# Scratch words of the integer conversions in one of three product banks, beside the first expert

## The chip, the cores and the metric

The kernel runs on one core of one Trainium2 chip. The metric is the device time of the whole program in microseconds (us), the median of three runs. The engines are PE (matmul), DVE (vector), ACT (scalar), POOL (GpSimd) and SP (which issues most DMAs). Each runs its own instructions in order and waits on semaphores for the others.

## The reference

Three layers follow one another: a linear attention with decay, a mixture of eight experts that each take exactly 384 tokens, and a dense layer with a rational function between its two products. Tokens are handed to experts greedily, best score first.

```python
for t in range(S):                                    # attention, S = 768, 4 x 8 heads of 64
    state = gamma * state + einsum('bhd,bhe->bhde', k[:, :, t], v[:, :, t])
    y[:, :, t] = scale * einsum('bhd,bhde->bhe', q[:, :, t], state)
...
for idx in np.argsort(-(x @ w_gate).flatten()):       # routing, cap = 3072 / 8 = 384
    tok, e = idx // E, idx % E
    if assigned[tok] < 0 and counts[e] < cap: assigned[tok] = e; counts[e] += 1
...
out[mask] = np.maximum(x[mask] @ w1[e], 0) @ w2[e]    # D = 512, F = 1024
...
h = x @ w_in                                          # 512 -> 2048
g = (a0 + a1*h + a2*h**2 + a3*h**3) / (1 + |b0|*|h| + |b1|*h**2 + 1e-6)
return g @ w_out                                      # 2048 -> 512
```

`w_in` and `w_out` arrive as 64-bit floats, and the kernel converts them to 32-bit words itself.

## The kernel before, in words

The attention and the gate run first (to about 190 us). The rest goes expert by expert, `n` = 0 to 7, and each expert's 384 tokens pass through all four products before the next expert's. An expert has three stages here. `xt` turns the gathered tokens round (three tiles). The first layer alternates `mm1(n, f)` and `mm2(n, f)` for eight blocks f, the third alternates `mm3(n, i)` and `mm4(n, i - 3)` for sixteen blocks i. Every 32-bit product is three matmuls of a high and a low part (`three`), and one product of this size is 12 matmuls.

Between the third and the fourth product lies the rational function: `rat1` (ACT L868 to L870, POOL L871, DVE L872 and L873), `rat2` (ACT L882, L883), `rat3` (DVE L888 to L890) and `gsplit` (ACT L895, POOL L896), which gives `mm4` its operand `hg`. DVE L873 is the last reader of the product that `mm3` left in PSUM.

PSUM has eight banks: `pr` for the routing, four `acc` for `mm2` and `mm4`, and three of the name "w", which `xt`, `mm1` and `mm3` take in turn.

Two more jobs run beside the first expert. The routing of the next expert is a chain of small steps that goes back and forth between DVE and PE in bank `pr` (L628 and L641 on PE, L635 to L637, L650, L583, L592 and L598 on DVE). And twelve blocks of `w_out` and `w_in` that weren't converted during the attention are converted now: six beside the first layer (`job_conv`, L949) and six beside the third (`in_conv_a`, L970). Twenty others were converted during the attention. One conversion (`conv`) is a shift and mask on DVE (L241), a scaled copy of the low words on ACT (L242), an OR on DVE (L243) and an addition on DVE (L244, in the rows as CUSTOM_DVE_ANT_0), after which ACT and POOL split the result (L247, L248). The conversions during the attention keep the intermediate word t1 in a PSUM tile `cvp`. The twelve beside the first expert keep it in SBUF, in the tile of the result (`xg` or `w2r`).

The order of PE, ACT and POOL is that of the code. The order of DVE and SP is made by a scheduler, which has its own idea of times and of when a buffer comes free.

## Time and profile before

| | |
|---|---|
| Time, median of 3 runs | 1081.24 us (1080.59 to 1082.49) |
| The profiled execution: its own time | 1081.6 us |
| Its span, first to last instruction | 1079.7 us |
| PE busy | 1010.1 us (94%) |
| DVE / ACT / POOL busy | 775.5 / 698.5 / 629.1 us |
| First expert: first layer | about 202 to 248 us |
| First expert: third layer | about 248 to 323 us |

The profile is one execution, some 0.4 us above the median. Starts in it are microseconds from the first instruction. In a row of the timeline, the bracket at the end is the idle time of that engine before the row and what ended it.

### The profile page before, as it was taken

What the parts mean: (1) busy time and instruction counts of PE and PEld (TensorE: products, weight loads), DVE (VectorE), ACT (ScalarE), POOL (GpSimd) and SP (SyncE); (2) the same over time, 40 slices, a digit from 0 to 9 for tenths busy, and PEclk for the clock granted to TensorE, in tenths of its full rate; (3) what the DMA queues carried; (4) which work ended last, traced back from release to release, by engine and by line L of the source; (5) the groups of instructions that cost most, each with busy time, mean ns of one, the idle gap of its engine ahead of it and who ended that gap; (6) DMA issues with size and microseconds to landing.
All of it is one profiled execution on the core that took longest, in us unless ns stands there. A gap on an engine that the chain in (4) does not pass through costs nothing.

```text
span 1079.7 us, 18280 instructions
## 1 busy us (share of the span) xinstructions
PE 1010.1 (94%) x6278; PEld 922.2 (85%) x6278; DVE 775.5 (72%) x1862; ACT 698.5 (65%) x1365; POOL 629.1 (58%) x612
## 2 busy tenths in 40 slices
PE   6999885679889999999999999999999999999995
PEld 5888774678779989998999899999998999989984
DVE  4899887678994788478747874787578756751773
ACT  6889882346684488458745874587358736873883
POOL 5677662464686367635663666366736663666452
PEclk9999997699999999999999999999999999999998
DMA  9999862523333212321232124212422142223110
GB/s 191 244 250 252 226 162 89 151 93 96 100 127 118 88 50 79 117 88 59 69 121 86 59 69 127 79 59 70 137 69 68 60 137 70 88 65 110 50 59 29
DMA packets 142028, 115.01 MB, mean 107 GB/s; under 512 B 56560, under 2 KB 122352, under 8 KB 141936
## 3 DMA queue, kind: packets, MB, share of 16 engines
q1 hardware_dynamic: 131184, 76.10, 26.7%
q0 software_dynamic: 10752, 37.75, 10.5%
q8 instruction: 49, 0.80, 0.3%
q14 instruction: 43, 0.35, 0.1%
HBM read 98.10 MB, written 15.73 MB: 105 GB/s over the span
## 4 chain that ended last, share of the span: by engine, by line
PE 63%; DVE 7%; ACT 2%; issue 2%; POOL 1%; POOLq 0%; DVEq 0%
PE w L814 30%; PE acc L910 22%; PE acc L814 8%; PE pr L628 1%; PE w L798 1%; DVE hg L825 1%; DVE cm L592 1%; ACT hg L824 0%; DVE t L872 0%; DVE t L890 0%; POOL qq L871 0%; DVE yT L842 0%; DVE qq L888 0%; DVE acc L889 0%; DVE pr L583 0%
## 5 line engine op out<-in xcount | busy, mean ns | idle before, releaser
L910 PE MATMUL acc<-woh,hg 128*128 128x512 f32 x1152 | 290.2, 397 | 4.8 <-ACT hg L895 4.5
L910 PEld LDWEIGHTS acc<-woh,hg 128*128 128x128 f32 x1152 | 212.8, 188 | 49.7 <-ACT hg L895 7.0
L871 POOL TENSOR_TENSOR qq<-qq,z 128x384 f32<-128x384 f32 x127 | 129.4, 1019 | 165.2 <-ACT z L869 163.7
L814 PE MATMUL w<-yT,wih 128*128 128x384 f32 x960 | 179.6, 339 | 0.1
L896 POOL TENSOR_TENSOR hg<-t,hg 128x384 fp32r<-128x384 f32 x127 | 131.6, 1037 | 81.4 <-ACT hg L895 53.1
L814 PEld LDWEIGHTS w<-yT,wih 128*128 128x128 f32 x960 | 166.4, 188 | 3.8 <-DVE yT L842 0.7
L814 PE MATMUL w<-xT,w1s 128*128 128x384 f32 x768 | 149.7, 343 | 0.6 <-ACT xT L800 0.6
L814 PE MATMUL acc<-hg,w2s 128*128 128x384 f32 x768 | 146.2, 339 | 0.3 <-DVE hg L825 0.3
L814 PEld LDWEIGHTS w<-xT,w1s 128*128 128x128 f32 x768 | 135.4, 192 | 1.9 <-ACT xT L800 0.8
L814 PEld LDWEIGHTS acc<-hg,w2s 128*128 128x128 f32 x768 | 132.7, 188 | 1.1 <-DVE hg L825 0.6
L888 DVE SCALAR_TENSOR_TENSOR qq<-qq,acc 128x384 f32<-128x384 f32 x128 | 70.8, 553 | 60.4 <-ACT acc L883 33.3
L248 POOL TENSOR_TENSOR w1s<-w1r,w1s 128x512 fp32r<-128x512 f32 x64 | 83.2, 1300 | 49.2 <-ACT w1s L247 48.4
L814 PE MATMUL w<-yT,wis 128*128 128x384 f32 x576 | 110.0, 339 | 1.1 <-DVE t L873 1.1
L248 POOL TENSOR_TENSOR w2s<-w2r,w2s 128x512 fp32r<-128x512 f32 x64 | 83.2, 1301 | 43.7 <-ACT w2s L247 43.4
L895 ACT ACTIVATE hg<-t 128x384 fp32r<-128x384 f32 x128 | 67.1, 525 | 63.9 <-DVE t L890 63.7
L814 PEld LDWEIGHTS w<-yT,wis 128*128 128x128 f32 x576 | 100.3, 188 | 3.7 <-DVE t L873 1.3
L868 ACT ACTIVATE qq<-w,rb 128x384 f32<-128x384 f32 x128 | 73.3, 573 | 36.9 <-PE w L814 35.6
L824 ACT ACTIVATE hg<-w 128x384 fp32r<-128x384 f32 x64 | 31.4, 490 | 92.1 <-PE w L814 92.1
L870 ACT ACTIVATE t<-w,ab 128x384 f32<-128x384 f32 x128 | 86.1, 673 | 0.0
L872 DVE TENSOR_TENSOR t<-w,t 128x384 f32<-128x384 f32 x128 | 70.4, 550 | 21.1 <-ACT t L870 21.1
L247 ACT ACTIVATE w2s<-w2r 128x512 fp32r<-128x512 f32 x64 | 40.2, 629 | 68.1 <-issue 41.7
L825 DVE SCALAR_TENSOR_TENSOR hg<-w,hg 128x384 fp32r<-128x384 f32 x64 | 35.6, 556 | 66.3 <-ACT hg L824 66.0
(183 smaller groups left out, 1761.7 us busy)
## 6 DMA issues: line engine op xcount, KB each, us to landing
wis<-wid POOLq DMA_DIRECT2D x42, 512.0 KB, 3.5
w1r<-in_moe_w_dram SPq DMA_DIRECT2D x64, 256.0 KB, 2.8
w2r<-in_moe_w_dram SPq DMA_DIRECT2D x64, 256.0 KB, 2.7
qn<-in_q_dram SPq DMA_DIRECT2D x48, 128.0 KB, 4.1
kn<-in_k_dram SPq DMA_DIRECT2D x24, 256.0 KB, 4.6
vn<-in_v_dram SPq DMA_DIRECT2D x24, 256.0 KB, 5.0
xd<-xn SPq DMA_DIRECT2D x48, 128.0 KB, 3.9
raw<-in_moe_w_in_dram SPq DMA_DIRECT2D x10, 512.0 KB, 6.5
```

The lines of the kernel that those rows point to most:

```text
L247: nc.scalar.activation(dst[:, 0], src, AF.Copy)
L248: lo_eng.tensor_tensor(dst[:, 1], src, dst[:, 0].bitcast(F32), op=OP.subtract)
L814: nc.tensor.matmul(o, w[a], x[b], start=first and n[key] == 1, stop=last and n[key] == total)
L825: HLO[n, f] = nc.vector.scalar_tensor_tensor(h[:, 1], p, 0.0, h[:, 0].bitcast(F32), op0=OP.max, op1=OP.subtract).ins
L868: nc.scalar.activation(qq, p, AF.Square, scale=rb)
L870: nc.scalar.activation(t, p, AF.Identity, bias=ab[:, 2:3], scale=ab[:, 3:4])
L871: light(n, i).tensor_tensor(qq, qq, z, op=OP.add)
L872: nc.vector.tensor_tensor(t, p, t, op=OP.mult)
L888: nc.vector.scalar_tensor_tensor(qq, qq, QC, r, op0=OP.add, op1=OP.mult)
L895: nc.scalar.activation(g[:, 0], t, AF.Copy)
L896: light(n, i).tensor_tensor(g[:, 1], t, g[:, 0].bitcast(F32), op=OP.subtract)
L910: nc.tensor.matmul(ACC[t], g[:, x, t * 128:(t + 1) * 128], woh[:, i, y], start=i == 0 and x + y == 0, stop=i == NF2 - 1 and x == 1)
```

## The change

The conversions beside the first expert put the intermediate word t1 into a PSUM tile of a new name, "x", with one buffer. The three product banks are now two of the name "w" and this one. While the first expert runs, `mm1` and `mm3` get "w" alone, and so take turns with two banks; the third tile of `xt(0)` and the tiles of `xt(1)` go to "x". From the second expert on, every third product goes to "x", so that products again take turns with three banks.

```diff
+    WN = [0]
+
+    def wtile(shape, first=False):
+        if not first:
+            WN[0] += 1
+        x = not first and WN[0] % 3 == 0
+        return ps.tile(shape, F32, name="x" if x else "w", bufs=1 if x else 2)
+
+    def ctile():
+        return ps.tile([128, 512], I32, name="x", bufs=1)
+
     def xt(n, t):
...
-        p = ps.tile([128, KD, 128], F32, name="w", bufs=3)
+        p = ps.tile([128, KD, 128], F32, name="x", bufs=1) if n == 1 else wtile([128, KD, 128])
...
     def mm1(n, f):
-        p = ps.tile([128, CAP], F32, name="w", bufs=3)
+        p = wtile([128, CAP], n == 0)
...
     def mm3(n, i):
-        p = US[n, i] = ps.tile([128, CAP], F32, name="w", bufs=3)
+        p = US[n, i] = wtile([128, CAP], n == 0)
...
     def job_conv(j):
-            conv(rawx[:, j % 3], CA[j], mp.tile([128, KD * 128], I32, name="xg", bufs=TB))
+            conv(rawx[:, j % 3], CA[j], mp.tile([128, KD * 128], I32, name="xg", bufs=TB), ctile())
...
     def in_conv_a(j):
-        conv(RX[j], CA[j], mp.tile([128, KD * 128], I32, name="w2r"))
+        conv(RX[j], CA[j], mp.tile([128, KD * 128], I32, name="w2r"), ctile())
```

PE, ACT, POOL and SP issue the same instructions in the same order as before; the only differences are in DVE's order, and they begin in the first expert's first layer and end at the second expert's start. Lines of the changed kernel from `xt` on are 13 higher than before (L873 of before is L886).

DVE in the first layer, at the fourth conversion, before (`cmk`, `ce`, `ex` and `fs` belong to the routing, `hg` is the first layer's result):

```order
L825 SCALAR_TENSOR_TENSOR hg<-w,hg 128x384
L635 TENSOR_TENSOR cmk<-pr,cft 64x128
L241 TENSOR_SCALAR xg<-yT 128x512
L636 TENSOR_REDUCE ce<-cmk 64x16
L243 SCALAR_TENSOR_TENSOR xg<-yT,xg 128x512
L637 TENSOR_TENSOR ex<-ce,pr 64x128
```

The same place after the change:

```order
L838 SCALAR_TENSOR_TENSOR hg<-w,hg 128x384
L635 TENSOR_TENSOR cmk<-pr,cft 64x128
L241 TENSOR_SCALAR x<-yT 128x512
L636 TENSOR_REDUCE ce<-cmk 64x16
L243 SCALAR_TENSOR_TENSOR x<-yT,x 128x512
L637 TENSOR_TENSOR ex<-ce,pr 64x128
```

Nothing moved; L241 and L243 write, and L243 reads, the bank "x" where it was `xg` in SBUF.

DVE in the third layer, where the routing's L635 falls between blocks 8 and 9, before:

```order
L888 SCALAR_TENSOR_TENSOR qq<-qq,acc_3739 128x384
L889 SCALAR_TENSOR_TENSOR acc_3739<-qq,acc_3739 128x384
L890 SCALAR_TENSOR_TENSOR t<-t,ab,acc_3739 128x384
L635 TENSOR_TENSOR cmk<-pr,cft 64x128
L872 TENSOR_TENSOR t<-w,t 128x384
L636 TENSOR_REDUCE ce<-cmk 64x16
L873 SCALAR_TENSOR_TENSOR t<-t,ab,w 128x384
```

The same place after the change:

```order
L901 SCALAR_TENSOR_TENSOR qq<-qq,acc_3749 128x384
L902 SCALAR_TENSOR_TENSOR acc_3749<-qq,acc_3749 128x384
L903 SCALAR_TENSOR_TENSOR t<-t,ab,acc_3749 128x384
L885 TENSOR_TENSOR t<-w,t 128x384
L244 ISA w2r<-x,w2r 128x1024
L635 TENSOR_TENSOR cmk<-pr,cft 64x128
L886 SCALAR_TENSOR_TENSOR t<-t,ab,w 128x384
```

A conversion's addition came forward between them, and L635 still stands ahead of the last reader of product 9 (L873, now L886). Product 11 on PE waits for that reader in the changed kernel; before, it waited for the reader of product 8.

## Rows read from the trace of the kernel before

**Rows 1.** Stretches of the span: busy us of each engine, granted PE clock, DMA.

```profile
core 0: us, PE busy (x) PEld busy (x) DVE busy (x) ACT busy (x) POOL busy (x), PEclk, DMA share, GB/s
30.00:171.00 141.00, 127.97 (x1380) 114.74 (x1379) 125.43 (x240) 122.01 (x260) 93.02 (x78) 1.00 0.89 216
202.00:248.00 46.00, 39.46 (x209) 37.95 (x210) 33.27 (x81) 18.03 (x34) 26.45 (x19) 0.91 0.31 95
215.00:230.00 15.00, 9.87 (x58) 8.87 (x58) 12.81 (x25) 7.16 (x13) 11.12 (x9) 1.00 0.52 172
230.00:235.00 5.00, 5.00 (x22) 4.90 (x23) 2.87 (x10) 1.01 (x2) 1.18 (x2) 0.66 0.20 56
248.00:323.00 75.00, 66.86 (x346) 57.68 (x345) 70.62 (x158) 56.81 (x112) 48.85 (x47) 1.00 0.37 116
323.00:430.00 107.00, 106.30 (x580) 97.41 (x579) 78.08 (x206) 67.68 (x131) 62.40 (x64) 1.00 0.27 84
```

**Rows 2.** What PE waited for, 202 to 324 us: total us, times, longest.

```profile
PE pr L641 <- DVE ex L637: 4.2, 3, 2.9
PE acc L910 <- ACT hg L895: 3.6, 5, 1.5
PE pr L628 <- DVE pr L598: 3.3, 2, 1.9
PE w L798 <- DVE xT L801: 1.6, 1, 1.6
```

**Rows 3.** Instructions on tile cvp (attention): ns min/median/max, first and last start.

```profile
L241 DVE TENSOR_SCALAR cvp<-raw x20: 676/684/697, 30.9 to 168.4; 128x512 int32<-128x512 int32 x20
L243 DVE SCALAR_TENSOR_TENSOR cvp<-raw,cvp x20: 675/685/696, 37.0 to 169.1; 128x512 int32<-128x512 int32 x20
L244 DVE CUSTOM_DVE_ANT_0 cv<-cvp,cv x20: 674/680/693, 37.7 to 170.1; 128x1024 uint16<-128x1024 uint16 x20
```

**Rows 4.** Instructions on tile xg (first layer), columns as above.

```profile
L241 DVE TENSOR_SCALAR xg<-yT x6: 408/839/1481, 210.0 to 240.0; 128x512 int32<-128x512 int32 x6
L243 DVE SCALAR_TENSOR_TENSOR xg<-yT,xg x6: 692/1092/1657, 210.4 to 240.5; 128x512 int32<-128x512 int32 x6
L244 DVE CUSTOM_DVE_ANT_0 xg<-xg x6: 673/810/1570, 212.3 to 242.6; 128x1024 uint16<-128x1024 uint16 x6
```

**Rows 5.** DVE groups, 250 to 312 us: busy us, mean ns, idle before.

```profile
L243 DVE SCALAR_TENSOR_TENSOR w2r<-w2s,w2r 128x512 int32<-128x512 int32 x6 | 5.4, 896 | 0.0
L244 DVE CUSTOM_DVE_ANT_0 w2r<-w2r 128x1024 uint16<-128x1024 uint16 x6 | 5.1, 858 | 0.0
L241 DVE TENSOR_SCALAR w2r<-w2s 128x512 int32<-128x512 int32 x6 | 3.2, 530 | 0.5 <-DMA w2s<-in_moe_w_in_dram 0.5
L583 DVE SCALAR_TENSOR_TENSOR pr<-ni,cit 128x16 int32<-128x16 int32 x1 | 3.0, 3025 | 0.0
```

**Rows 6.** Timeline of PE: start, us, line, xcount, idle before.

```profile
217.26 0.40 PE L628 MATMUL pr<-cm,ohr 128*64 128x128 f32 x3 [1.93 <-DVE pr L598]
...
222.44 2.25 PE L814 MATMUL w<-xT,w1s 128*128 128x384 f32 x12
...
229.87 0.33 PE L641 MATMUL pr<-ex,oner 128*128 128x128 f32 x1 [2.87 <-DVE ex L637]
230.04 3.43 PE L814 MATMUL w<-xT,w1s 128*128 128x384 f32 x12
...
275.51 2.27 PE L814 MATMUL w<-yT,wis 128*128 128x384 f32 x12
...
296.07 0.34 PE L628 MATMUL pr<-cm,ohr 128*64 128x128 f32 x3
```

**Rows 7.** Timeline of DVE, same columns.

```profile
214.46 1.34 DVE L241 TENSOR_SCALAR xg<-yT 128x512 int32<-128x512 int32 x1
...
226.45 1.48 DVE L241 TENSOR_SCALAR xg<-yT 128x512 int32<-128x512 int32 x1 [0.45 <-POOL woh L248]
...
228.13 1.49 DVE L243 SCALAR_TENSOR_TENSOR xg<-yT,xg 128x512 int32<-128x512 int32 x1
...
278.59 0.60 DVE L873 SCALAR_TENSOR_TENSOR t<-t,ab,w 128x384 f32<-128x384 f32 x1
...
296.63 0.28 DVE L635 TENSOR_TENSOR cmk<-pr,cft 64x128 f32<-64x128 f32 x1
```

**Rows 8.** Source line L583, all its executions: ns min/median/max.

```profile
L583 DVE SCALAR_TENSOR_TENSOR pr<-ni,cit x7: 171/183/3025, 203.1 to 795.5; 128x16 int32<-128x16 int32 x7
```

## The prediction

> **What bounds the kernel now.** I read the stretches first. From 323 us on PE is busy 106.30 of 107 us, and the later experts look alike, so nothing that the change does there can matter: products take turns with three banks as before. Beside the first expert PE is not full: it idles 46 - 39.46 = 6.5 us in the first layer and 75 - 66.86 = 8.1 us in the third [rows 1]. Those 14.7 us are what can be won, and since PE runs without a break afterwards, a microsecond won or lost before 323 us arrives whole at the end of the kernel.

> Second, what PE waits for there. Nearly all of it comes from DVE: L637 and L598, steps of the routing (4.2 and 3.3 us), `hg` of L895, which ACT makes right behind DVE's L890 (3.6 us), and L801 (1.6 us) [rows 2]. In the third layer DVE is busy 70.62 of 75 us [rows 1]: it is the bound. In the first layer it is busy only 33.27 of 46 us, but the routing goes back and forth between DVE and PE, and a routing step that stands behind a slow conversion makes PE wait.

> Third, the conversions themselves. With the intermediate word in PSUM (attention) the three DVE instructions take 676 to 697, 675 to 696 and 674 to 693 ns, twenty times each [rows 3]. With the word in SBUF (first layer) the same ones take 408 to 1481, 692 to 1657 and 673 to 1570 ns [rows 4]. POOL is as busy in the first place (93 of 141 us, 66%) as in the second (26.45 of 46 us, 57%) [rows 1]. So it isn't that POOL is idle in the attention; what differs is that L243 and L244 have both inputs in SBUF, and that L241 runs from SBUF to SBUF, at its best in 408 ns.

> **The change part by part.** The conversions: I take the medians of [rows 3] for their new durations, since those rows are the same instructions with the same operands in the same memories. L241 loses its fast case (408 to 684) and all three lose their slow cases.

> [...]

> First layer, three terms:

> 1. The longest wait. PE stands 2.87 us before 229.87, for L637 [rows 6]. Ahead of L637 on DVE are L241 (1.48 us, after 0.45 us of waiting for POOL's split of an earlier conversion, which still read that SBUF tile) and L243 (1.49 us) [rows 7]. With 0.68 and 0.69 us, 1.6 us go; the 0.45 us go too, since L241 now writes a bank that POOL never reads. Sum 2.05 us; 0.8 us of the wait stays.
> 2. The wait of 1.93 us before 217.26, for L598 [rows 6]. L241 at 214.46 stands in front: 1.34 becomes 0.68 us [rows 7], and the L243 and L244 before it (up to 1657 and 1570 ns [rows 4]) end some 0.2 us earlier where ACT's low words let them. 0.85 us.
> 3. The clock. [...] Five us at 0.66 cost 1.7 us of work at full speed. With 0.8 us left of the wait I expect no fall: 1.7 us. Bounds: 0 if it falls at another place, 1.7.

> The smaller waits of the same two kinds (1.4 and 0.3 us are what remains of [rows 2] in this layer) may shrink by a few tenths, and the first conversion of the third layer, which now has 0.68 for 0.43 us ahead of an L637, gives some back. I leave both out. `mm1` with two banks costs nothing here: two products of one kind are a whole `mm1` and `mm2` apart (over 4 us), and L825 has read the bank by then. First layer: 2.05 + 0.85 + 1.7 = 4.6 us.

> Third layer, four terms:

> 4. DVE is the bound, so its time counts. Six conversions take 6 x (896 + 858 + 530) ns = 13.7 us [rows 5] and would take 6 x (685 + 680 + 684) ns = 12.3 us [rows 3]. Gain 1.4 us.
> 5. L583, a routing step of 16 elements with two SBUF inputs, took 3.02 us here [rows 5]; its median over seven executions is 183 ns [rows 8]. It stood ahead of the L801 for which PE waited 1.6 us [rows 2]. The change doesn't touch it, but its neighbours on POOL shift, and by that median another such stall is the exception. Of the 2.8 us I count what PE saw, 1.6 us. Bounds: 0 if it or its like is caught again, 2.8.
> 6. The shorter lead. With three banks PE ran ahead: product 7 began at 275.51, while L873 read product 5 up to 278.59 + 0.60 = 279.19 [rows 6, 7]. With two banks it can't begin before, 3.7 us later. But PE then finds `hg` ready, for which it stood 3.6 us in total [rows 2]: the wait moves from `mm4` to `mm3` as long as DVE is the bound. Net cost 0.1 us; bounds 0 and 3.7.
> 7. A new handshake. L635 waits for PE's L628 and stands ahead of L873 of product 9, for which PE's product 11 waits now. L628 begins at 296.07 [rows 6], L635 ends at 296.63 + 0.28 = 296.91, L873 takes 0.60 (0.52 after the overlap with the instruction ahead) [rows 7]: PE could go on at about 297.4 where it went on at 296.25, right behind L628. Cost 1.2 us, once. The other routing steps of this layer have more room, since DVE's L873 stands ahead of them or is older.

> `xt(1)` waits for the last conversion and for its own earlier tile in "x"; the conversion's L244 stands ahead of the L650 that PE's previous step feeds, so I count nothing. Third layer: 1.4 + 1.6 - 0.1 - 1.2 = 1.7 us.

> Sum: 4.6 + 1.7 = 6.3 us. The profiled execution took 1081.6 us, so 1075.3 us for one like it, and 0.36 us less for the median: **1074.9 us**.

> **The rivals.**

> *Little is left.* The fall of the clock only moves (term 3 is 0), terms 1 and 2 come (2.9 us), and the third layer pays them back: the lead costs most of its 3.7 us, since PE's last blocks lose it without DVE being late, against 1.4 us of term 4. 2.9 + 1.4 - 3.5 = 0.8 us: 1080.4 us. For it: DVE idles only 4.4 us in that layer [rows 1], so PE and DVE are close to even there. Against it: the waits of `mm4` on `hg` show that PE had more lead than it could use.

> *Slower: the two banks tie PE and DVE together.* The handshake of term 7 needs a routing step on PE between two products. PE makes nine such steps between products of the third layer, by its order. If each cost 1.2 us, that is 10.8 us against 7.6 us of gains (terms 1 to 5): 1081.2 + 3.2 = 1084.4 us. It decides from the seventh step on (7 x 1.2 = 8.4 us). Against it: in the order of DVE I see the pattern, L635 or its like between L872 and the L873 for which the next product waits, once.

> *More.* PE's waits on DVE vanish in the first layer (6.5 + 1.7 us) and all of terms 4 and 5 arrive (4.2 us): 12.4 us, 1068.8 us. Against it: L244 waits for ACT's L242 in any case, and the routing keeps its path.

> That the change doesn't act is not a rival: the operands in DVE's order show "x".

> **How the numbers follow.** No difference means here within 0.2% (2.2 us), about what a measurement of this kernel can tell. The forecast (gain of 2.2 to 10 us) has 0.74, *more* 0.06, *little is left* 0.13, *slower* 0.07. So faster 0.80, same 0.13, slower 0.07. The range reaches down to 1069.5, into *more*, and up to 1080.8, past the middle of *little is left*; about 0.06 lie below and 0.13 above.

> **What would show it.** L241, L243 and L244 beside the first expert within 670 to 700 ns (terms 1, 2, 4). The wait before the L641 near 229 us under 1 us, and the clock at 1.00 from 215 us on (term 3). The waits of L910 on `hg` gone, and in their place waits of L814 on L873 of about the same sum, with one of about 1.2 us behind the L628 near 293 us (terms 6, 7). No execution of L583 over 1 us (term 5). PE full from about 317 us on. The prediction is wrong if the waits on L873 sum to more than 10 us, if another instruction with two SBUF inputs (L667, L696, L732) takes over the lost time, or if the clock falls elsewhere.

## The result, and the profile after

The changed kernel takes 1072.09 us (median of 4 runs, 1072.01 to 1074.42) against 1080.91 us of the kernel before beside it: a ratio of 0.9915, 95% interval 0.99 to 0.9929, so 8.8 us less. The forecast was 1074.9 us. The profiled execution took 1072.1 us, its span 1070.2 us.

Stretches of the changed kernel (engines and columns as in [rows 1]):

```profile
202.00:248.00 46.00, 42.08 (x235) 40.05 (x236) 32.58 (x94) 21.02 (x40) 24.54 (x20) 0.95 0.39 118
230.00:235.00 5.00, 5.00 (x31) 4.99 (x29) 3.75 (x12) 2.21 (x4) 3.58 (x3) 1.00 0.00 0
248.00:323.00 75.00, 70.96 (x367) 62.50 (x366) 68.52 (x160) 59.34 (x116) 51.32 (x51) 1.00 0.34 106
323.00:430.00 107.00, 106.30 (x581) 97.39 (x580) 77.45 (x200) 67.69 (x130) 62.61 (x64) 1.00 0.27 85
```

PE has 2.6 us more work in the first of these stretches and 4.1 us more in the third: work of the next stretch that has moved up. From 323 us on nothing has changed. The granted clock in 230 to 235 us is 1.00 where it was 0.66.

What PE waited for, 202 to 324 us (columns of [rows 2]):

```profile
PE w L827 <- DVE t L886: 3.9, 5, 1.4
PE pr L628 <- DVE pr L598: 2.1, 2, 1.0
PE pr L641 <- DVE ex L637: 1.8, 2, 1.1
PE w L827 <- ACT xT L813: 0.6, 1, 0.6
```

The waits on `hg` and at the tiles of `xt(1)` (L798 in [rows 2]) are gone, and the routing's have about halved. L886, the last reader of a product, makes PE wait five times; in the kernel before it (as L873) did so once, at the product behind the first tile of `xt(1)`. That wait and the one ahead of this tile, in the kernel before:

```profile
PE w L814 <- DVE t L873: 1.1, 1, 1.1
PE w L798 <- DVE fs L650: 0.4, 1, 0.4
```

The conversions in the first layer (columns of [rows 4]), and the groups of DVE from 240 to 307 us with the third layer's six (columns of [rows 5]):

```profile
L241 DVE TENSOR_SCALAR x<-yT x6: 675/686/690, 209.7 to 234.2; 128x512 int32<-128x512 int32 x6
L243 DVE SCALAR_TENSOR_TENSOR x<-yT,x x6: 676/695/695, 210.4 to 234.9; 128x512 int32<-128x512 int32 x6
L244 DVE CUSTOM_DVE_ANT_0 xg<-x,xg x6: 683/692/693, 212.0 to 237.1; 128x1024 uint16<-128x1024 uint16 x6
...
L243 DVE SCALAR_TENSOR_TENSOR x<-w2s,x 128x512 int32<-128x512 int32 x6 | 4.1, 686 | 0.1
...
L583 DVE SCALAR_TENSOR_TENSOR pr<-ni,cit 128x16 int32<-128x16 int32 x1 | 1.0, 1040 | 0.0
```

PE's timeline at the places of [rows 6], at the start of the third layer (243.33), and at the second expert's first product (313.96):

```profile
216.07 0.40 PE L628 MATMUL pr<-cm,ohr 128*64 128x128 f32 x3 [1.04 <-DVE pr L598]
...
226.07 0.33 PE L641 MATMUL pr<-ex,oner 128*128 128x128 f32 x1 [0.72 <-DVE ex L637]
226.23 2.32 PE L827 MATMUL w<-xT,w1s 128*128 128x384 f32 x12
...
243.33 2.30 PE L827 MATMUL w<-yT,wih 128*128 128x384 f32 x12
...
289.86 0.34 PE L628 MATMUL pr<-cm,ohr 128*64 128x128 f32 x3
291.34 2.35 PE L827 MATMUL w<-yT,wis 128*128 128x384 f32 x12 [1.14 <-DVE t L886]
...
313.96 2.24 PE L827 MATMUL w<-xT,w1s 128*128 128x384 f32 x12
```

In the kernel before, the second expert's first product began at 323.36 us, so the first expert gave 9.4 us; the two profiled executions differ by 9.5 us (1081.6 and 1072.1).

### The profile page after: what moved, and what is told of

Same layout as the page of the kernel before. It is cut to its first block, busy times and chain, and to the rows that moved or that the text cites. A ratio compares the mean times of both kernels' runs of the same rounds, so it can differ in the third digit from the quotient of the medians.

```text
span 1070.2 us, 18273 instructions
## 1 busy us (share of the span) xinstructions
PE 1007.2 (94%) x6278; PEld 920.4 (86%) x6278; DVE 767.4 (72%) x1862; ACT 698.6 (65%) x1365; POOL 623.7 (58%) x612
## 4 chain that ended last, share of the span: by engine, by line
PE 74%; DVE 11%; ACT 6%; issue 3%; DMA 3%; POOL 1%; SPq 1%; POOLq 0%; DVEq 0%; ACTq 0%
PE w L827 23%; PE acc L923 23%; PE x L827 10%; PE acc L827 8%; DMA qn<-in_q_dram 2%; PE pa L382 2%; PE py L411 1%; PE pt L352 1%; PE pr L628 1%; PE pt L424 1%; PE py L407 1%; DVE cm L592 1%; ACT QB L365 1%; DVE hg L838 1%; ACT qt L364 1%
## 5 line engine op out<-in xcount | busy, mean ns | idle before, releaser
L827 PE MATMUL acc<-hg,w2s 128*128 128x384 f32 x768 | 145.9, 339 | 0.3 <-DVE hg L838 0.3
L827 PEld LDWEIGHTS acc<-hg,w2s 128*128 128x128 f32 x768 | 132.3, 188 | 1.1 <-DVE hg L838 0.6
L827 PE MATMUL w<-yT,wih 128*128 128x384 f32 x624 | 117.9, 340 | 0.9 <-DVE t L886 0.8
L827 PE MATMUL w<-xT,w1s 128*128 128x384 f32 x600 | 116.1, 342 | 0.6 <-ACT xT L813 0.6
L827 PEld LDWEIGHTS w<-yT,wih 128*128 128x128 f32 x624 | 108.1, 188 | 3.6 <-DVE t L886 1.8
L827 PEld LDWEIGHTS w<-xT,w1s 128*128 128x128 f32 x600 | 105.3, 191 | 1.9 <-ACT xT L813 0.8
L895 ACT ACTIVATE z<-qq,qcb 128x384 f32<-128x384 f32 x128 | 77.7, 607 | 8.0 <-POOL qq L884 8.0
L827 PE MATMUL w<-yT,wis 128*128 128x384 f32 x408 | 78.1, 339 | 3.1 <-DVE t L886 3.1
L903 DVE SCALAR_TENSOR_TENSOR t<-t,ab,acc 128x384 f32<-128x384 f32 x128 | 78.4, 613 | 3.4
L827 PEld LDWEIGHTS w<-yT,wis 128*128 128x128 f32 x408 | 70.9, 188 | 5.8 <-DVE t L886 4.1
L902 DVE SCALAR_TENSOR_TENSOR acc<-qq,acc 128x384 f32<-128x384 f32 x128 | 71.6, 560 | 3.3
L896 ACT ACTIVATE acc<-z 128x384 f32<-128x384 f32 x128 | 63.5, 496 | 4.1
```

The costliest lines, as they stand in the source:

```text
L827: nc.tensor.matmul(o, w[a], x[b], start=first and n[key] == 1, stop=last and n[key] == total)
L895: nc.scalar.activation(z, qq, AF.Ln, bias=qcb)
L896: nc.scalar.activation(r[:, :CAP], z, AF.Exp, scale=-1.0)
L902: nc.vector.scalar_tensor_tensor(r, qq, 2.0, r, op0=OP.subtract, op1=OP.mult, reverse0=True)
L903: nc.vector.scalar_tensor_tensor(t, t, ab[:, 0:1], r, op0=OP.add, op1=OP.mult)
```

## The experiments

From PE's timeline two times are read for each kernel, in one profile each: the first layer, from the first `mm1` of the first expert to its first `mm3`, and the third layer, from there to the second expert's first `mm1`. The last column has the median time of all runs of a kernel and its ratio to runs of the kernel before beside them. Where an edit leaves a stage alone, the stage's time still differs between profiles by some 0.4 us (46.46 to 46.80 us for the first layer of before, 3, 5, 7 and 8); only the second kernel's first layer lies further off (last section).

| kernel | first layer | third layer | L583 in it | time, ratio (95%) |
|---|---|---|---|---|
| before | 46.80 | 74.59 | 3.02 | |
| changed | 41.30 | 70.63 | 1.04 | 1072.09, 0.9915 (0.99 to 0.9929) |
| 1 first layer only | 41.69 | 74.43 | 3.00 | 1076.44, 0.9953 (0.9941 to 0.9965) |
| 2 third layer only | 47.94 | 70.53 | 1.04 | 1077.93, 0.9962 (0.995 to 0.9974) |
| 3 two banks only | 46.58 | 71.71 | 0.85 | 1078.78, 0.9976 (0.9966 to 0.9985) |
| 4 own word in SBUF | 45.85 | 74.83 | 2.99 | 1079.84, 0.9989 (0.9978 to 1.0001) |
| 5 `ni` in PSUM | 46.46 | 72.60 | 0.17 | 1080.8, 0.9983 (0.9973 to 0.9993) |
| 6 changed, small steps in PSUM | 41.52 | 70.83 | 0.17 | 1071.94, 0.9905 (0.9891 to 0.9919) |
| 7 three banks, xt(1) apart | 46.75 | 73.51 | 0.17 | 1081.3, 0.9997 (0.9987 to 1.0007) |
| 8 two banks, xt(1) in turn | 46.64 | 74.91 | 0.80 | 1082.79, 1.0005 (0.9995 to 1.0015) |
| 9 POOL fills zeros | 40.63 | 74.77 | 3.03 | 1076.05, 0.9949 (0.9937 to 0.9961) |
| 10 changed, all steps later | 41.55 | 73.05 | 1.04 | 1075.97, 0.9943 (0.993 to 0.9956) |
| 11 as 10 and 6 | 41.16 | 73.02 | 0.17 | 1074.62, 0.9934 (0.9921 to 0.9947) |
| 12 changed, one step later | 41.65 | 70.50 | 1.13 | 1072.27, 0.9913 (0.9899 to 0.9928) |

### 1 to 3: the two halves, and the banks without the words

Of the changed kernel, the first leaves out what concerns the third layer, the second what concerns the first, the third both uses of `ctile()` (the words in SBUF, the banks as changed).

```diff
 1, 3      in_conv_a:  - conv(RX[j], ..., ctile())      + conv(RX[j], ...)
 2, 3      job_conv:   - conv(rawx[...], ..., ctile())  + conv(rawx[...], ...)
 1         mm3, xt(1): + p = wtile(...)                 (three banks, xt in turn)
 2         mm1:        + p = wtile([128, CAP])
```

> Only the six conversions beside the first layer put their word into PSUM, and only mm1 of the first expert takes turns with two banks; the third layer keeps three banks and its words in SBUF. Theory (the conversions no longer contend with POOL's reads): first layer 5.4 us shorter as in the changed kernel, third layer as before within 1 us, so 5 us in all (ratio 0.995). Rival (the gain is the scheduler's new order of DVE): DVE's order in the first layer hardly changes, so under 1.5 us.

> Only the six conversions beside the third layer put their word into PSUM, with two banks for mm3 of the first expert; the first layer is as before. Theory: 2 to 4 us shorter, all after 248 us, and the wait for L637 near 229 us and the clock's fall stay. If the two layers add up, this and the first-layer kernel together give the 8.8 us of the whole change. Rival (the third layer's gain was that L583 happened not to be caught): it is caught again or not, and the gain is 0 or 3.

> Two banks for the products of the first expert, as in the changed kernel, but the words stay in SBUF, so bank x is almost unused. Theory: the shorter lead costs 1 to 4 us against before (waits of PE on L873 in place of those on hg, and the handshake behind L628), so 1082 to 1085 us. Rival (turns of two are themselves the gain, since PE no longer runs ahead of DVE): faster than before by 2 us or more.

The halves add up: 0.47% and 0.38%, 0.85% together, as the whole change. The first layer's half is all the words; mere banks leave that layer as it was (46.58). In the third layer banks and words are both worth something: 74.59 to 71.71 us by the banks, 1.1 us more by the words. The third kernel missed its expectation (1 to 4 us slower): it is 0.24% faster. Part of what its banks give is that L583 takes 0.85 us there in place of 3.02; the fifth kernel prices that.

### 4 and 9: is it PSUM, or POOL's subtractions?

The fourth takes the kernel before and gives the intermediate word an SBUF tile of its own. The ninth keeps the words of the kernel before, and the low parts that POOL subtracts for the weights `w1s`, `w2s` and `woh` during the first layer are filled with zeros instead (they are left out of the result): POOL then writes SBUF there and reads none.

```diff
 4  job_conv, in_conv_a: + conv(..., mp.tile([128, 2, KD * 128], I32, name="wis" or "w1s")[:, 0])
 9  split:               + nc.gpsimd.memset(dst[:, 1].bitcast(F32), 0.0)   # first layer, for the subtraction
```

> Three banks as before; the word gets an SBUF tile of its own (a part of buffers that lie idle at that time), so L241 doesn't wait for POOL's split of an earlier conversion any more, but L243 and L244 still have two SBUF inputs and L241 still goes from SBUF to SBUF. Theory: those waits were 0.9 us in all, so at most 1 us is gained, and the durations keep their spread up to 1.5 us. Rival (it was the reuse of the tile that held DVE up): 4 us or more.

> The kernel before, all words in SBUF, three banks, the same order on VectorE; only GpSimd's low parts of the weights that are split during the first expert's first layer (the subtractions into w1s, w2s and woh) are replaced by a fill with zeros, so those low parts are left out of the result and GpSimd reads no SBUF there. If the conversions were slow because GpSimd's two-input subtractions held them up: L243 and L244 fall from means of 896 and 858 ns to 670 to 700 ns with a largest below 800 while they stand between 202 and 248 us, the 2.87-us wait of the first layer falls to about 0.7 to 1.0 and the layer from 46.8 to 41 to 43 us; the third layer stays at 74 to 75 us and L583 at 3.0; the time 1075 to 1078 us. If the gain came from the PSUM word as such, whatever GpSimd does: L243 and L244 keep their spread to 1.5 us, the first layer stays at 46 to 47 us and the time within 0.1% of the kernel before.

The fourth gains 0.11%, its interval reaching to no gain, as its theory had it, and the spread stays (source lines on the tile of the word, first layer):

```profile
L243 DVE SCALAR_TENSOR_TENSOR wis<-yT,wis x6: 693/1481/1665, 212.3 to 241.0; 128x512 int32<-128x512 int32 x6
L244 DVE CUSTOM_DVE_ANT_0 xg<-wis,xg x6: 766/996/1554, 214.3 to 243.1; 128x1024 uint16<-128x1024 uint16 x6
```

In the ninth it goes, with both inputs of L243 and L244 still in SBUF:

```profile
L241 DVE TENSOR_SCALAR xg<-yT x6: 406/421/425, 209.5 to 233.4; 128x512 int32<-128x512 int32 x6
L243 DVE SCALAR_TENSOR_TENSOR xg<-yT,xg x6: 674/692/1660, 209.9 to 233.9; 128x512 int32<-128x512 int32 x6
L244 DVE CUSTOM_DVE_ANT_0 xg<-xg x6: 683/693/694, 211.8 to 236.4; 128x1024 uint16<-128x1024 uint16 x6
```

The one slow L243 stood beside the one subtraction that still fell into its way; DVE's and POOL's timelines of the same kernel:

```profile
209.94 1.66 DVE L243 SCALAR_TENSOR_TENSOR xg<-yT,xg 128x512 int32<-128x512 int32 x1
```

```profile
209.58 1.48 POOL L253 TENSOR_TENSOR w1s<-w1r,w1s 128x512 fp32r<-128x512 f32 x1 [1.31 <-ACT w1s L249]
210.99 0.54 POOL L251 MEMSET w2s<- 128x512 f32 x1
```

So it is POOL's subtractions that hold the two-input conversions up, and PSUM helps because the word is then not read from SBUF: in the changed kernel 17 of the 18 conversion instructions of this layer run beside a subtraction, in part or whole, and none takes over 695 ns; L583, in the fifth kernel below, falls from 3.02 to 0.17 us when its input `ni` moves to PSUM. That POOL's fills, which only write SBUF, don't hold these conversions up rests on two instructions of the ninth, since few fills met a conversion: the L243 above ended 0.54 us behind the subtraction with a fill beside it nearly to its end, and an L244 at 222.22 us took 0.69 us with 0.28 us of a fill beside it. L241 has one SBUF input, and while it wrote SBUF it was held too (up to 1481 ns [rows 4], 425 ns at most in the ninth); what held it, no run here shows. The ninth's layer came out 0.4 us below the 41 to 43 us that I expected, and its one slow L243 lies above the 800 ns that I had set as the largest.

### 5 and 6: L583

```diff
 5  + pni = prb[:, 296:297].bitcast(I32)          # prb: the routing's PSUM bank
 5  + L582, L583 use pni (n > 0) where they used ni
 6  the same on the changed kernel, and the small tiles S and A of the routing in prb
```

> The kernel before, with one change: the routing's one-word tile ni, which L583 reads beside a table in SBUF, lies in a free column of bank pr, so L583 has one SBUF input. DVE's order is all but that of before. Theory (third layer: L583's 3 us stall was a term of 1.6 us): L583 takes 0.2 us, the third layer is 1.6 to 2.8 us shorter than the 74.6 us of before. Rival (the stall was hidden): no change.

> The changed kernel, and three small tiles of the routing (ni, S, A) in free columns of bank pr from the second route on, so that L583, L667, L671 and L672 have one SBUF input each. Theory: their 1.04, 0.75 and 0.50 us fall to about 0.2 each, DVE gains some 1.8 us in the third layer, and since DVE is still near its bound there 0.5 to 1.8 us arrive: 1070.3 to 1071.6 us. Rival (PE is the bound by now): no change.

With `ni` in PSUM, L583 (now L585) never stalls; its seven executions from 202 us on, in the fifth kernel:

```profile
L585 DVE SCALAR_TENSOR_TENSOR pr<-pr,cit x7: 173/176/183, 202.7 to 792.6; 128x16 int32<-128x16 int32 x7
```

The third layer falls by 2.0 us, the time by 0.17%. On the changed kernel the same brings nothing that shows, where I expected 0.5 to 1.8 us (70.83 against 70.63 us, the intervals of the ratios overlap): PE waits for nothing there from 291.34 to 324 us, and L583 begins at 302.06, so nothing of PE stood behind it any more.

### 7 and 8: two banks, and the tiles of xt(1)

Both take the third kernel (no words in PSUM). The seventh gives `mm3` three banks up to block 10 and leaves xt(1) alone in "x", the eighth gives `mm3` two and lets xt(1) take turns with it.

```diff
 7  - p = US[n, i] = wtile([128, CAP], n == 0)   + p = US[n, i] = wtile([128, CAP], n == 0 and i >= 11)
 8  - p = ps.tile(..., name="x", bufs=1) if n == 1 else wtile([128, KD, 128])   + p = wtile([128, KD, 128], n == 1)
```

> Words in SBUF as before; mm3 of the first expert takes turns with three banks up to block 10 and with two from then on, and the tiles of xt(1) have bank x to themselves. Theory A (the two-banks kernel gained because xt(1) no longer takes its turn among the products): about 2.9 us shorter in the third layer, as there. Theory B (it gained because DVE's new order keeps the instructions with two SBUF inputs off POOL's reads): only as much as L583 and its like happen to shrink, which this order doesn't promise.

> As the two-banks kernel (words in SBUF), but the tiles of xt(1) take their turn in the two banks, so x lies idle in the third layer; DVE's order is that of the two-banks kernel but for five rows. Theory A: the gain in the third layer is gone, 74 us or more. Theory B: the gain stays, about 72 us, and L583 stays at about 1 us or less.

What PE waited for most, 202 to 324 us, in the third kernel and then in the eighth:

```profile
PE w L827 <- DVE t L886: 5.4, 7, 1.2
```

```profile
PE w L827 <- DVE t L886: 7.6, 10, 1.7
```

The three more are the products behind the tiles of xt(1), in the eighth:

```profile
308.44 2.35 PE L827 MATMUL w<-yT,wis 128*128 128x384 f32 x12 [1.67 <-DVE t L886]
...
313.74 2.35 PE L827 MATMUL w<-yT,wih 128*128 128x384 f32 x12 [0.41 <-DVE t L886]
...
319.04 2.35 PE L827 MATMUL w<-yT,wis 128*128 128x384 f32 x12 [0.21 <-DVE t L886]
```

Two banks that `xt` shares are no better than three (74.91 against 74.59 us, although L583 stalls 2.2 us less); with xt(1) apart the same two are 3.2 us faster. The fifth kernel, in which L583 doesn't stall, is the fairer measure: against its 72.60 us the two banks alone lose 2.3 us (0.6 of DVE's time is L583 there), xt(1) apart with three banks (73.51, L583 at 0.17) loses 0.9, and both together (71.71) win 0.9. So the gain is in the pair. The seventh kernel missed the 2.9 us of its theory A: it wins 1.1 us in the layer and nothing that shows in the time, since one product, the first that has two banks, waits 1.82 us for L886, and the clock falls behind it (the product takes 3.35 us; the mean clock from 248 to 323 us is 0.98).

### 10 to 12: the routing steps behind the reader of the product

The changed kernel, with the routing steps that are dealt out behind `mm4` put behind the L873 (there L888) of the block before: all of them (10), all of them with the edits of 6 (11), and only the one for which PE's product 11 waited (12).

```diff
     mm4(n, i - LAG)
-    slot(1)
+    with tc.issue_after(R1[0, i - 1]) if n == 0 else ExitStack():      # 12: if n == 0 and i == 10
+        slot(1)                                                         # R1: L873 of block i
```

> The changed kernel, with the routing steps that are dealt out between the first expert's third-layer blocks put behind the last accumulation (L873) of the block before on VectorE's queue. If the 1.14-us wait of product 11 on L886 is the routing operation L635 that stands ahead of it in the queue: the wait falls below 0.3 us, the third layer from 70.63 to 69.5 to 70.0 us and the time to about 1071.0 us, unless PE's small routing products now wait longer for VectorE (the steps stand later), which is the rival: then L628, L641 or L910 wait 1 us or more where they waited nothing, the third layer stays at 70.4 to 71.5 us and the time within 0.1% of the changed kernel's 1072.1 us. If the two banks themselves tie PE to VectorE at every block: waits of L827 on L886 grow in number and the third layer is above 72 us.

> The changed kernel with one input of the small routing operations in PSUM (as in the earlier run on the changed kernel, which took 1071.9 us) and the later place of the routing steps. If both leave something on the path: the third layer below 70 us and 1070.3 to 1071.3 us. If VectorE no longer bounds the third layer: 70.4 to 71 us in that layer and a time within 0.1% of 1072 us.

> The changed kernel with one routing step of the first expert put later on VectorE's queue: the L635 for which PE's product 11 waited (1.14 us before 291.34 us) stands behind the L886 of block 9 instead of ahead of it; every other step stays where it was. If that order is the handshake of the prediction: the wait before product 11 falls below 0.3 us, no other wait grows by more than 0.3 us, the third layer goes from 70.63 to 69.4 to 69.9 us and the time to about 1071.0 us. If the step only moves what VectorE owes to the next product, as when all the steps were put later: product 12 or a small routing product behind it waits about 1 us more, the third layer stays at 70.4 to 71 us and the time within 0.1% of the changed kernel's 1072.1 us.

None of the tenth's three expectations came whole. The wait before product 11 is gone, as the first had it, but product 10, which waited for nothing in the changed kernel, now waits 2.24 us. The layer is above 72 us, as the last had it, but PE waits on L888 five times, as often as in the changed kernel on L886. PE's timeline there:

```profile
284.28 2.26 PE L925 MATMUL acc<-woh,hg 128*128 128x512 f32 x9
288.79 3.58 PE L827 MATMUL w<-yT,wih 128*128 128x384 f32 x12 [2.24 <-DVE t L888]
292.17 2.61 PE L925 MATMUL acc<-woh,hg 128*128 128x512 f32 x9
```

The steps bunch up. From 284.77 us DVE ran L563 to L567 and L592 (the changed kernel has these by 282 us) ahead of the L888 for which PE waited until 288.79. The clock falls behind that wait (0.85 from 290 to 300 us). The eleventh goes the same way (2.26 us of waiting, 73.02 us) and missed both its expectations, 71 us or less.

The twelfth is the clean one: a single step changes its place. Its PE, and its DVE around the same product:

```profile
291.01 0.34 PE L628 MATMUL pr<-cm,ohr 128*64 128x128 f32 x3
292.35 2.35 PE L827 MATMUL w<-yT,wis 128*128 128x384 f32 x12 [1.00 <-DVE t L888]
```

```profile
290.62 0.55 DVE L887 TENSOR_TENSOR t<-w,t 128x384 f32<-128x384 f32 x1
291.09 0.68 DVE L244 CUSTOM_DVE_ANT_0 w2r<-x,w2r 128x1024 uint16<-128x1024 uint16 x1
291.69 0.60 DVE L888 SCALAR_TENSOR_TENSOR t<-t,ab,w 128x384 f32<-128x384 f32 x1
292.21 0.28 DVE L635 TENSOR_TENSOR cmk<-pr,cft 64x128 f32<-64x128 f32 x1
```

L635 is behind L888 and the wait is 1.00 in place of 1.14 us, where the first expectation had less than 0.3. The layer (70.50 us) and the time are as the other had them, but without the further wait of about 1 us that it named. The routing step was not what PE waited for. In the changed kernel's DVE, at the same place, it is seen too:

```profile
287.71 0.55 DVE L901 SCALAR_TENSOR_TENSOR qq<-qq,acc 128x384 f32<-128x384 f32 x1 [0.37 <-POOL hg L909]
...
289.90 0.68 DVE L244 CUSTOM_DVE_ANT_0 w2r<-x,w2r 128x1024 uint16<-128x1024 uint16 x1
290.50 0.27 DVE L635 TENSOR_TENSOR cmk<-pr,cft 64x128 f32<-64x128 f32 x1
290.69 0.60 DVE L886 SCALAR_TENSOR_TENSOR t<-t,ab,w 128x384 f32<-128x384 f32 x1
```

PE's L628 ended at 290.20, L635 began at 290.50 without waiting, and from 287.71 on DVE ran without a gap up to L886. It was simply behind, by its own work and by 0.37 us of waiting; the conversion's L244, which the scheduler had brought forward, takes 0.60 us of the queue (289.90 to 290.50), L635 0.19. No run moves L244 alone.

## Why the prediction was right, and where its terms were off

**The first layer: right, by its own steps.** It forecast 4.6 us and 5.5 came. Term 1: 2.87 to 0.72 us, 2.15 (forecast 2.05). Term 2: 1.93 to 1.04 us, 0.89 (0.85). Term 3: that the clock wouldn't fall behind 0.8 us of waiting was my estimate; behind the 0.72 us that were left it stayed at 1.00 from 226 to 235 us, in place of the 0.66 from 230 to 235 us that the term prices, and the product took 2.32 us. Before, 6.01 us lay between the product at 230.04 and the next `mm1` at 236.05; now 4.61 us lie between 226.23 and 230.84: 1.4 us (1.7 from the average clock). The smaller waits, which I left out, gave 0.7 (1.41 to 1.05 and 0.33 to nothing), and the layer's second product was 0.3 us shorter (2.65 to 2.31 us) at the rising clock (0.84 to 0.95 from 206 to 209 us), which is luck. The premise is confirmed: with the word in PSUM the conversions take 675 to 695 ns, L241 included, which lost its 408 ns. A PSUM source costs L243 next to nothing here: its median is 692 ns from SBUF alone with zero fills on POOL (kernel 9) and 695 ns with a PSUM source.

**The third layer: right in sign, 1.7 us forecast, 4.0 measured.** One chain of the kernels above splits it: before to 5 (L583), 5 to 3 (two banks and xt(1) apart), 3 to changed (words). Each step is a difference of two profiles, and L583 still takes 0.85 us in 3.

| step | forecast | measured in the layer |
|---|---|---|
| term 4, conversions | -1.4 | -1.1 (71.71 to 70.63) |
| term 5, L583 | -1.6 | -2.0 (74.59 to 72.60) |
| terms 6 and 7, two banks, and xt(1) in a bank of its own | +1.3 and 0 | -0.9 (72.60 to 71.71) |

**The mis-sized step** is the sentence "so I count nothing" on xt(1). Its tiles wait for nothing, as forecast; but I asked what they would wait for, not what they had been in the way of. Before, PE waited 0.44 us ahead of the first of them, 1.05 us at the product behind it and 1.65 us ahead of the second. The last is term 5's and goes with L583's stall (kernel 5); the first two stay there (0.38 and 1.10 us) and go wherever xt(1) has its own bank (2, 3, 6, 7, 10 to 12, changed). From before to changed the layer's waits at xt(1) fall from 3.14 us to nothing, 3.97 us on `hg` become 3.94 on L886, and the routing's stay (1.03 and 1.08). So 1.5 of the 2.3 us that this layer gave beyond the forecast are the two waits that I left out (the rows put the shorter one down to L650, a step of the routing; why it ends that wait is open); the other 0.8 us lie in PE's time outside its waits (66.45 to 65.61 us), and their cause is open. Left in turn in two banks, the tiles would have cost 3.2 us (kernel 8 against 3).

**Term 5 came for another reason than I gave.** I called the stall of L583 an exception by its median [rows 8]. It isn't chance: with the banks of before in the third layer it took 3.02, 3.00, 2.99 and 3.03 us (before, 1, 4, 9). It goes where the order of that stretch is another (0.17 to 1.13 us in 2, 3, 7, 8, 10, 12 and changed). My sign, "no execution over 1 us", was missed by 0.04 us.

**Term 7 had the size and not the cause.** 1.2 us were forecast and 1.14 came, in the very place, and that was luck: the round trip PE, L635, L886 that I priced is not what made the wait, as kernel 12 shows: without it 1.00 us stay. The likely cause, by the timeline, is that DVE was behind. Term 6 was right: `hg`'s waits of 4.0 us in kernel 5 are 4.2 us on L886 in kernel 3, its product 11 (1.18) left out, so 0.2 us more where 0.1 was forecast.

**The rivals.** *Little is left* fell with the clock and the layer. *Two banks tie PE and DVE together* is refuted: one routing step stood where it was feared, and moving it took 0.14 us from the wait (kernel 12). Kernel 8, as slow as before, does wait 7.6 us on L886, but the 2.3 us that it has above kernel 3 lie at xt(1)'s tiles, not at routing steps, and its words are in SBUF. *More* didn't come; kernel 6, in which L583 takes 0.17 us where it took 1.04 in the changed kernel, gave nothing beyond the interval.

## What to carry to other kernels

When one engine's instructions may be holding another's up, look at the spread of one instruction's durations and not at its mean (L243 here: 693 to 1665 ns in kernel 4, 676 to 695 ns in the changed one), and put each slow execution beside the timeline of the other engine; moving one operand to the other memory can then pay even where the best case gets slower (L241 here, 408 to 675 ns). When a buffer pool is divided, price what the moved tiles stood in the way of, not only what they will wait for. A wait that appears where it was forecast is not proof of its cause: move the suspect alone and look whether the wait goes with it.

## What the runs showed of the hardware that was not expected

```profile
307.47 3.02 DVE L583 SCALAR_TENSOR_TENSOR pr<-ni,cit 128x16 int32<-128x16 int32 x1
310.41 0.54 DVE L888 SCALAR_TENSOR_TENSOR qq<-qq,acc 128x384 f32<-128x384 f32 x1
```

```profile
307.22 1.01 POOL L896 TENSOR_TENSOR hg<-t,hg 128x384 fp32r<-128x384 f32 x1
308.19 1.01 POOL L871 TENSOR_TENSOR qq<-qq,z 128x384 f32<-128x384 f32 x1
309.17 1.28 POOL L248 TENSOR_TENSOR wis<-w2r,wis 128x512 fp32r<-128x512 f32 x1
```

It got through only when the third of three subtractions and additions that followed each other without a gap had ended, not after the first.

The clock's answer to a wait was not the same in every profile. Behind the same wait of 1.93 us before the same L628, the product took 2.30 to 2.32 us in five kernels (before, 3, 5, 7, 8; clock 0.99 to 1.00 from 215 to 230 us), 3.86 us in the fourth and 3.69 us in the second (0.89 in both), whose instructions up to there are those of before but for the bank:

```profile
217.91 0.58 PE L628 MATMUL pr<-cm,ohr 128*64 128x128 f32 x3 [1.93 <-DVE pr L598]
218.29 3.69 PE L827 MATMUL w<-xT,w1s 128*128 128x384 f32 x12
```

Behind 1.44 us in the changed kernel it stayed (2.35 us), behind 1.82 us in the seventh it fell (3.35 us). So a first layer of 47.94 us in the second kernel, whose profiled run is the slowest of its six, says nothing against its edit; its ratio over all runs, 0.38% or 4.1 us, is what its third layer gained (74.59 to 70.53).
